# Order of the second block's weight loads and the transposed gradient tiles on one DMA queue

## The chip, the cores and the metric

One core of a Trainium2 chip runs the whole program in one launch. The metric is the device time of one execution in microseconds; the kernel before takes 1849.81 us (median of three runs, 1849.18 to 1849.89).

## The reference

The program computes a layer and all its gradients (a `vjp`). With x = A_q (2048 rows of 1024, bf16):

```
xn  = layernorm(x)
A   = xn * (longconv(kv, ssm_k) + kv * ssm_D),   kv = shortconv(k, shift_k) * v
B   = (relu(xn @ W_gate) * (xn @ W_up)) @ W_down            # 1024 -> 3584 -> 1024
out = x + A + B
grads of (A_q, A_k, A_v, shift_k, ssm_k, ssm_D, W_gate, W_up, W_down) for grad_out
```

## The kernel before, in words

TensorE (PE) works through branch B, and the matmuls of branch A (a long convolution by transforms) are woven in between from about 120 us on. Only the first 60 us matter for the change. They belong to `hidden`, which computes the hidden layer and its gradient in 14 blocks: two halves of the rows (8 tiles of 128 rows each) times 7 blocks of 512 hidden columns. A block `n` makes, for each row tile `s`,

- `gate` (tile `ps_g`): 8 matmuls of xnT[s], the transposed normalised rows, with `wg`, a block of W_gate in four pieces of 256 KB;
- `up` (`ps_u`): 8 matmuls of xnT[s] with `wu`, the block of W_up, likewise four pieces;
- `grad_row` (`ps_h`): 8 matmuls of goT[s], the transposed rows of grad_out, with `wdT`, the transposed block of W_down, four pieces again, of which piece q serves matmuls 2q and 2q + 1.

The results go over ScalarE and VectorE to the tiles `ru`, `ht` and `gh` and are stored as `h_d` and `ug_d`. A tile xnT or goT stays in its slot for all 7 blocks of a half, so these are loaded once, in the first block.

The first block (`n == 0`, `ahead` in the code) runs while the layernorm is still being made, row tile after row tile. xnT 0 to 5 are transposed on PE (`flip_xn`), xnT 6 and 7 by a DMA transpose from the layernorm's output in SBUF (`flip_xn`, last queued one kept in `self.turned`). All eight goT are DMA transposes from HBM (`load_T`): 0 to 3 are asked for before `hidden` begins, 4 to 7 in the loop over `sp`. The order of row tiles on PE, from 32.8 us, is: gradient of tiles 2, 3, 4, 5; gate and up of 6; gate and up of 7; gradient of 6 and 7. Then block 2 (`n == 1`) starts with gate of tiles 0 and 1, up of 0 and 1, gradient of 0 and 1.

There are four sets of weight buffers. The first block uses three of them. The second block's gate weights go into the spare set, so their load waits for no matmul. Its up weights go where the first block's gate weights were and its down weights where the first block's up weights were, so these loads wait for PE.

Nearly all loads are on the queue of SyncE (SP), which issues them one after the other. In the first block the stores of h, of the gradients and of xn go over GpSimd (POOL). The order on a queue comes from priorities that the code counts up (`Pri`), from pins to program order, and from `issue_after(ins)`, which places the instructions traced inside its block behind `ins` where both are on the same engine. In the kernel before, the lines are

```
while len(gT) < min(sp + 4, HS):
    with self.tc.issue_after(self.turned.ins if sp == 4 else self.copied.ins):
        gT.append(self.load_T(g, len(gT), "goT", HS + len(gT)))
```

where `self.copied` is a copy on ScalarE or VectorE, and further down `load_gate()` behind `self.stored`, which in the first block is a store on POOL. So the queue of SP holds in this stretch: goT 2, 3, the small load `sk_b`, wg (4 pieces), goT 4, 5, xnT 6, 7, goT 6, 7, wu (4), wdT (4).

Of the kernel before, what the change touches and what calls it, by code (L numbers as in the profile page):

```python
# [17 lines left out]
P = 128  # L18
# [30 lines left out]
class ABranch:  # L49
# [47 lines left out]
    def load(self, out, in_):  # L97
        self.pri.now()
        ins = self.nc.sync.dma_start(out=out, in_=in_)
        if self.pin:  # L100
            self.tc.keep_in_program_order(ins)
        else:
            self.pri.pin(ins)
# [776 lines left out]
class LnMlp:  # L880
# [292 lines left out]

    def load_T(self, src, st, name, slot, always=False):
        t = self.act_tile(name, slot)
        self.pri.pin(self.nc.sync.dma_start_transpose(out=t[:].rearrange("p (a b) -> p a b", b=P),
                                                      in_=src[st * P:(st + 1) * P, :]), always=always)
        return t

    def load_nat(self, src, st, name, slot):  # L1180
# [40 lines left out]
    def hidden(self, first, goT, load, ln, tables, Wg, Wu, Wd, g, xn_d, h_d, ug_d):  # L1221
# [6 lines left out]
        for n in range(N):  # L1228
            half, fb = divmod(n, self.FB)
            s0, cols, ahead = half * HS, slice(fb * 512, fb * 512 + 512), n == 0  # L1230
# [13 lines left out]
            def load_gate():  # L1244
                if last:
                    self.slab_part(h_d, 0, "hs", self.hs, 4, sg)
                else:
                    nw[0] = self.col_block(Wg, nb, "wg", to[0])
# [5 lines left out]
            def load_down(q):  # L1254
                if last and q == 0:
                    self.slab_part(h_d, 0, "hs", self.hs, 0, spare)
                elif not last:
                    if q == 0:
                        nw[2] = []
                    nw[2].append(self.row_piece_T(Wd, nb, "wdT", to[2], q, n == 1))  # L1260
# [105 lines left out]
            def gate_up(sp):  # L1366
                end = sp == HS - 2
                if ahead and not end:
                    gate(sp)
                    yield from step(self.PACE[0])  # L1370

                    def turn():
                        flip(sp + 2)
                        with self.tc.issue_after(self.copied.ins):
                            chunk()
                    up(sp, None, {4: turn})
                    yield from step(self.PACE[1])
                    gate(sp + 1)
                    yield from step(self.PACE[0])
                    up(sp + 1)  # L1380
                    yield from step(self.PACE[1])
                    return
                rows = [(f, s) for f in (gate, up) for s in (sp, sp + 1)]
                for f, s in sorted(rows, key=lambda r: r[1]) if ahead else rows:
                    f(s)
                    yield from step(self.PACE[f is up])
                    if end and f is gate and s == sp + 1:
                        (load_up if ahead else load_gate)()
                if end and ahead:
                    for q in range(4):  # L1390
                        load_down(q)
                elif end:
                    load_up()
                if swap:
                    next_rows(sp)
# [8 lines left out]
            def last_rows(sp):  # L1404

                self.hold = self.busy = True
                for q in range(2):
                    load_down(sp // 2 + q)

                def run(f, s):  # L1410
                    f(s)
                    yield from step(self.PACE[f is up])
                yield from run(gate, sp)
                yield from run(gate, sp + 1)
                yield from run(up, sp)
                yield from run(gate, sp + 2)
                yield from run(gate, sp + 3)
                load_gate()
                yield from run(up, sp + 1)
                yield from grad_row(sp)  # L1420
                yield from run(up, sp + 2)
                yield from run(up, sp + 3)
                load_up()
                self.busy = swap and not last
                if n == 1:
                    chunk()
                if swap:
                    next_rows(sp)
                    next_rows(sp + 2)
                for s in range(sp + 1, HS):  # L1430
                    yield from grad_row(s)
                if swap:
                    next_grads(sp)
                    next_grads(sp + 2)
# [37 lines left out]
            def grad(sp):  # L1472
                for s in (sp, sp + 1):
                    at = 3 if sp == 0 else 0
                    yield from grad_row(s, {at: lambda: flip_ahead(sp)} if ahead and s == sp + 1 else {})
                if swap:
                    next_grads(sp)

            def chunk(steps=3):
                with self.tc.issue_after(self.ln_act.ins):  # L1480
                    for _ in range(steps):
                        next(ln)
# [7 lines left out]
            for sp in range(0, HS, 2):  # L1490
                self.pri.now()
                while len(gT) < min(sp + 4, HS):
                    with self.tc.issue_after(self.turned.ins if sp == 4 else self.copied.ins):
                        gT.append(self.load_T(g, len(gT), "goT", HS + len(gT)))
                if ahead or sp < HS - 4:
                    if not ahead:
                        load_down(sp // 2)
                        yield from gate_up(sp)
                        if n == 4 and sp == 2:
                            for k in filter(self.bare, range(HS)):  # L1500
                                xT[k] = self.load_T(xn_d, k, "xnT", k)
                        if sp:
                            self.hold = False
                        elif fb:
                            self.busy = False
                    if not ahead or sp != 4:
                        yield from grad(sp)
                    if ahead and sp == 2:
                        yield from grad(4)
                elif sp == HS - 4:  # L1510
                    yield from last_rows(sp)
                if ahead:
                    with self.tc.issue_after(self.stored.ins):
                        if sp == 0:
                            load_gate()
                if ahead and sp in (2, 6):
                    with self.tc.issue_after(self.put.ins):
                        for put in self.kept[0:4] if sp == 2 else self.kept[4:8]:
                            put()
                if ahead and sp == 6:  # L1520
                    with self.tc.issue_after(self.sent.ins):
                        load(6)
                if ahead and sp + 4 < HS:
                    yield from gate_up(sp + 4)
                if n == 1 and sp < 4:
                    with self.tc.issue_after(self.stored.ins):
                        for i in ((7,), (8, 9))[sp // 2]:
                            load(i)
                if n == 1 and sp != 4:
                    chunk()  # L1530
                if ahead and sp == 4:
                    with self.tc.issue_after(self.ln_act.ins), self.tc.issue_after(self.ln_dve.ins):
                        tables()
# [477 lines left out]
```

## Time and profile before

| | |
|---|---|
| median of three runs | 1849.81 us |
| lowest, highest | 1849.18, 1849.89 us |
| profiled execution: its own time | 1849.04 us |
| profiled execution: span | 1847.3 us |
| PE busy | 1827.6 us, 99% of the span |
| VectorE (DVE), ScalarE (ACT), POOL busy | 1118.2, 647.1, 34.9 us |
| DMA, mean over the span | 187 GB/s |
| SP's queue (q1) | 71.5% of 16 engines' span |
| PE by the table of stretches, 10 to 50 us | 39.79 of 40 us busy |

The profile is one execution. "SPq" rows are issues on SP's queue: start, then how long SP took to issue them. A number in square brackets is idle time of the engine before that row, with what ended it. A matmul of 128x512 is shown with 379 ns, since its row lasts until its results are out; one follows another every 0.216 us. The DMA share counts packets in flight on 16 engines and can be above 1.

### The profile page before, as it was taken

To read this page: it belongs to the slowest core of one execution; us is meant where nothing else is said; L and a number is where in the kernel's file an instruction comes from. 1 tells how busy PE (TensorE), PEld (TensorE's weight loads), DVE (VectorE), ACT (ScalarE), POOL (GpSimd) and SP (SyncE) were. 2 spreads that over 40 slices of the span, in tenths; PEclk is the share of its full clock that TensorE was granted. 3 is DMA by queue.
4 is the path that set the end of the run, shared out by engine and by line. 5 is a ranking of instruction groups with operands and counts; after the bars stand their busy time and mean duration, and the time that the engine had idled before them with its cause. 6 is when DMAs were issued, how large, how long until landed. Compare 5 with 4: busy or idle time off the path is not lost.

```text
span 1847.3 us, 32176 instructions
## 1 busy us (share of the span) xinstructions
PE 1827.6 (99%) x12970; PEld 846.9 (46%) x13182; DVE 1118.2 (61%) x1652; ACT 647.1 (35%) x1218; POOL 34.9 (2%) x72
## 2 busy tenths in 40 slices
PE   9999999999999999999999999999999999999999
PEld 4444444444444444444444444444444544444444
DVE  6656898698789758585685767721222222566652
ACT  6644544545444454544544455320000000111100
POOL 2200000000000000000000000000000000000000
PEclk9999999999999999999999999999999999999999
DMA  9997769969857866639566445389999767799973
GB/s 257 289 223 176 175 174 228 211 167 211 186 154 207 234 165 155 171 104 267 132 160 166 143 117 161 106 239 243 248 254 249 178 143 172 171 210 215 201 157 75
DMA packets 749989, 345.97 MB, mean 187 GB/s; under 512 B 581272, under 2 KB 718480, under 8 KB 749840
## 3 DMA queue, kind: packets, MB, share of 16 engines
q1 hardware_dynamic: 736048, 312.18, 71.5%
q10 hardware_dynamic: 9632, 17.04, 2.9%
q0 software_dynamic: 4160, 14.68, 2.3%
q8 instruction: 103, 1.69, 0.4%
q14 instruction: 46, 0.38, 0.1%
HBM read 143.79 MB, written 103.83 MB: 134 GB/s over the span
## 4 chain that ended last, share of the span: by engine, by line
PE 98%; issue 1%; DMA 0%; ACT 0%; SPq 0%; DVE 0%; ACTq 0%
PE ps_x L1860 21%; PE ps_w L1561 20%; PE ps_h L1152 10%; PE ps_u L1152 10%; PE ps_o L1728 10%; PE ps_g L1152 10%; PE ps_d L1561 9%; PE ps_c L83 4%; PE ps_d L1577 1%; PE ps_w L1577 1%; PE ps_r L1762 0%; DMA wg<-in_B_W_gate_dram 0%; DMA wu<-in_B_W_up_dram 0%; PE ps_u L1320 0%; ACT ln_j L965 0%
## 5 line engine op out<-in xcount | busy, mean ns | idle before, releaser
L1561 PE MATMUL ps_w<-ugs,xn_nat 128*128 128x512 bf16 x1675 | 375.2, 379 | 4.7 <-issue 2.9
L87 ACT CAST arena<-ps_c 128x512 bf16<-128x512 f32 x576 | 293.8, 611 | 103.0 <-PE ps_c L83 102.7
L1152 PEld LDWEIGHTS <-xnT 128*128 128x128 bf16 x1760 | 168.7, 98 | 205.2 <-issue 5.0
L1561 PEld LDWEIGHTS <-xn_nat 128*128 128x128 bf16 x1728 | 165.3, 98 | 200.8 <-issue 6.1
L343 DVE STREAM_TRANSPOSE arena<-arena 128x1024 f32<-128x1024 f32 x96 | 179.4, 1934 | 112.2 <-ACT arena L87 101.7
L1152 PE MATMUL ps_h<-wdT,goT 128*128 128x512 bf16 x873 | 201.9, 379 | 1.2
L1152 PE MATMUL ps_u<-wu,xnT 128*128 128x512 bf16 x861 | 201.3, 379 | 1.2
L1152 PE MATMUL ps_g<-wg,xnT 128*128 128x512 bf16 x848 | 199.4, 379 | 1.5
L1860 PE MATMUL ps_x<-wuT,guT 128*128 128x512 bf16 x878 | 197.5, 379 | 1.0
L1860 PE MATMUL ps_x<-wgT,ggT 128*128 128x512 bf16 x878 | 197.3, 379 | 0.9
L1878 ACT ACTIVATE w<-xn,m 128x512 f32<-128x512 bf16 x32 | 24.3, 806 | 479.9 <-DVE m L1871 366.6
L1728 PE MATMUL ps_o<-wd,hT 128*128 128x512 bf16 (+1 forms) x879 | 186.7, 372 | 0.9
L1561 PE MATMUL ps_d<-g_nat,hs 128*128 128x512 bf16 x743 | 166.5, 379 | 2.6 <-issue 1.9
L1860 PEld LDWEIGHTS <-guT 128*128 128x128 bf16 x896 | 87.7, 98 | 105.7
L1860 PEld LDWEIGHTS <-ggT 128*128 128x128 bf16 x896 | 87.7, 98 | 105.5
L1152 PEld LDWEIGHTS <-goT 128*128 128x128 bf16 x896 | 86.6, 98 | 104.3 <-issue 1.0
L1728 PEld LDWEIGHTS <-hT 128*128 128x128 bf16 x896 | 87.7, 98 | 99.9
L1449 ACT CAST gh<-ps_h 128x512 bf16<-128x512 f32 x112 | 66.2, 592 | 185.3 <-PE ps_h L1152 170.2
L1564 ACT CAST wi<-ps_w 128x512 bf16<-128x512 f32 x108 | 64.5, 597 | 187.6 <-PE ps_w L1561 149.1
L1720 DVE TENSOR_TENSOR ya<-ya,xe 128x1024 bf16<-128x1024 bf16 x16 | 11.1, 692 | 182.4 <-DMA xe<-xn_d 182.4
L91 DVE TENSOR_TENSOR t<-arena 128x2048 bf16<-128x2048 bf16 x96 | 114.0, 1220 | 0.4
L1561 PEld LDWEIGHTS <-hs 128*128 128x128 bf16 x768 | 73.3, 98 | 88.3 <-issue 1.8
(152 smaller groups left out, 1424.5 us busy)
## 6 DMA issues: line engine op xcount, KB each, us to landing
ugs<-ug_d SPq DMA_DIRECT2D x112, 256.0 KB
ug_d<-ru SPq DMA_DIRECT2D x104, 256.0 KB
wu<-in_B_W_up_dram SPq DMA_DIRECT2D x56, 256.0 KB
hs<-h_d SPq DMA_DIRECT2D x56, 256.0 KB
out_dram<-wi SPq DMA_DIRECT2D x56, 256.0 KB
wg<-in_B_W_gate_dram SPq DMA_DIRECT2D x55, 256.0 KB
h_d<-ht SPq DMA_DIRECT2D x104, 128.0 KB
gt<-in_grad_out_dram SPq DMA_DIRECT2D x32, 256.0 KB
```

What stands on the lines that cost most here:

```text
L83: self.pri.pin(self.nc.tensor.matmul(out, lhsT=lhsT, rhs=rhs, start=start, stop=stop))
L87: self.pri.pin(self.nc.scalar.copy(out=out, in_=in_))
L91: self.pri.pin(self.nc.vector.tensor_tensor(out=out, in0=in0, in1=in1, op=op))
L343: self.pri.pin(self.nc.vector.transpose(out=df[:, c0:c0 + 32, :], in_=sf[:, c0:c0 + 32, :]))
L1152: self.pri.pin(self.nc.tensor.matmul(ps[:], lhsT=xT[:, kt * P:(kt + 1) * P], rhs=w(kt), start=(kt == 0), stop=(kt == self.DT - 1)), always ...
L1449: self.pri.pin(nc.scalar.copy(out=gh[:], in_=ps[:]), **kept)
L1561: self.pri.pin(self.nc.tensor.matmul(ps[:], lhsT=lhsT(st), rhs=rhs(st), start=(st == 0), stop=(st == self.ST - 1)))
L1564: self.pri.pin(self.nc.scalar.copy(out=out, in_=ps[:]))
L1577: self.pri.pin(self.nc.tensor.matmul(ps[i][:], lhsT=lhsT(i, st), rhs=rhs(i, st), start=(st == 0), stop=(st == self.ST - 1)))
L1728: nc.tensor.matmul(ps, lhsT=hT[:, kt, :], rhs=self.wd[:, kt, oc], start=(kt == 0), stop=(kt == self.FT - 1))
L1860: nc.tensor.matmul(ps, lhsT=T[:, kt, :], rhs=W[:, kt, oc], start=(i == 0), stop=(i == n - 1))
L1878: nc.scalar.activation(out=w[:, oc], in_=xn[:, oc], func=ACT.Identity, scale=m[:, 7:8], bias=m[:, 6:7])
```

## The change

In the first block, goT 4 and 5 are now placed behind the previous goT load on SP (`self.loaded`, set in `load_T`), no longer behind a copy on another engine, which gave no order on SP. The four loads of the second block's gate weights move from behind a store on POOL at `sp == 0` to behind the last goT load at `sp == 4`. The queue of SP becomes: goT 2, 3, `sk_b`, goT 4, 5, xnT 6, 7, goT 6, 7, wg (4), wu (4), wdT (4). The instructions and their order on the other engines are those of before.

```diff
     def load_T(self, src, st, name, slot, always=False):
         t = self.act_tile(name, slot)
-        self.pri.pin(self.nc.sync.dma_start_transpose(out=t[:].rearrange("p (a b) -> p a b", b=P),
-                                                      in_=src[st * P:(st + 1) * P, :]), always=always)
+        self.loaded = self.nc.sync.dma_start_transpose(out=t[:].rearrange("p (a b) -> p a b", b=P),
+                                                       in_=src[st * P:(st + 1) * P, :])
+        self.pri.pin(self.loaded, always=always)
         return t
...
                 while len(gT) < min(sp + 4, HS):
-                    with self.tc.issue_after(self.turned.ins if sp == 4 else self.copied.ins):
+                    with self.tc.issue_after((self.turned if sp == 4 else self.loaded).ins):
                         gT.append(self.load_T(g, len(gT), "goT", HS + len(gT)))
+                if ahead and sp == 4:
+                    with self.tc.issue_after(self.loaded.ins):
+                        load_gate()
...
-                if ahead:
-                    with self.tc.issue_after(self.stored.ins):
-                        if sp == 0:
-                            load_gate()
```

## The prediction

> **What bounds the kernel now.** I read the page's busy table first, then the chain, then the window of the change. Bound: TensorE.
>
> ```profile
> PE 1827.6 (99%) x12970; PEld 846.9 (46%) x13182; DVE 1118.2 (61%) x1652; ACT 647.1 (35%) x1218; POOL 34.9 (2%) x72
> ...
> PE 98%; issue 1%; DMA 0%; ACT 0%; SPq 0%; DVE 0%; ACTq 0%
> ```
>
> The span is 1847.3 us and PE is busy for 1827.6, so 19.7 us are idle in all. The table by stretches says how little of that lies near the change:
>
> ```profile
> 0.00:10.00 10.00, 8.28 (x68) 1.00 0.84 279
> 10.00:50.00 40.00, 39.79 (x205) 1.00 1.12 261
> 50.00:100.00 50.00, 49.74 (x228) 1.00 1.08 268
> ```
>
> (Columns: stretch, its length, PE busy and matmuls, granted clock, DMA share, GB/s.) From 10 to 100 us PE is idle for 0.47 us at full clock, while the DMA engines' share is above 1. So here a DMA order can lose much and win little. The timeline of PE gives the moments at which each operand is wanted:
>
> ```profile
> 32.82 7.07 PE L1152 MATMUL ps_h<-wdT,goT 128*128 128x512 bf16 x31
> 39.89 1.90 PE L1152 MATMUL ps_g<-wg,xnT 128*128 128x512 bf16 x8
> ...
> 46.81 3.62 PE L1152 MATMUL ps_h<-wdT,goT 128*128 128x512 bf16 x16
> 50.26 3.62 PE L1152 MATMUL ps_g<-wg,xnT 128*128 128x512 bf16 x16
> 53.71 3.62 PE L1152 MATMUL ps_u<-wu,xnT 128*128 128x512 bf16 x15
> 57.17 3.62 PE L1152 MATMUL ps_h<-wdT,goT 128*128 128x512 bf16 x16
> ```
>
> Sixteen matmuls take 3.45 us from row to row (50.26 to 53.71), 0.216 us each. Block 2 begins at 50.26 with the moved weights. The weight loads of TensorE show the one wait:
>
> ```profile
> 39.88 6.59 PEld L1152 LDWEIGHTS <-xnT 128*128 128x128 bf16 x32 [0.49 <-DMA xnT<-ln_x]
> ```
>
> Tile 6 of the transposed activations comes late. The 32 matmuls from 32.82 would have ended their issue at 32.82 + 32 x 0.216 = 39.73; the next came at 39.89: 0.16 us lost. Last, SP's queue:
>
> ```profile
> 26.43 2.61 SPq L1144 DMA_DIRECT2D wg<-in_B_W_gate_dram  x4
> 29.09 5.46 SPq L1176 DMA_TRANSPOSE goT<-in_grad_out_dram  x2
> 34.66 2.79 SPq L1188 DMA_TRANSPOSE xnT<-ln_x  x2
> 37.51 3.65 SPq L1176 DMA_TRANSPOSE goT<-in_grad_out_dram  x2
> 43.98 2.45 SPq L1144 DMA_DIRECT2D wu<-in_B_W_up_dram  x4
> 46.52 8.30 SPq L1170 DMA_TRANSPOSE wdT<-in_B_W_down_dram  x4
> ```
>
> SP stands still from 41.16 to 43.98, waiting for PE to free wu's buffers. For landings I paired the completion counts that the trace records, sixteen per DMA and in order of issue: wg 30.91 to 34.04, goT 4 and 5 at 35.71 and 37.45, xnT 6 and 7 at 39.84 and 41.49, goT 6 and 7 at 43.79 and 44.97, wu 49.79, 50.52, 51.23, 52.24, wdT 53.69, 55.26, 55.95, 56.99.
>
> **The change part by part.** The instruction orders of the two programs are equal on PE, ACT, DVE and POOL, with nothing added or removed. On SP the four wg loads (256 KB each) go from ahead of goT 4 to behind goT 7; six transposed loads move up past them. Waits on landings follow the operands; no engine gets a new one on work.
>
> *goT 4 and 5 earlier.* Issued from 26.43 instead of 29.09. PE wants them at 36.27 and 38.00 (32.82 plus 16 and 24 matmuls); they landed 0.56 before. Nothing waited, so the gain is nothing.
>
> *xnT 6 and 7 earlier.* They also wait for DVE's scaling (L998), which ends at 33.14 and 35.71. So xnT 6 is issued at about 33.2 instead of 34.66 and lands near 38.4 (issue end to landing was 3.9 us: 35.95 to 39.84), before 39.73. The 0.16 us goes. What is late next is xnT 7: issued near 35.8 instead of 36.06, wanted at 43.35, landed at 41.49: 1.9 us to spare.
>
> *goT 6 and 7.* SP's gain shrinks to between the 0.3 us of xnT 7 and, because goT 6 and 7 took 2.05 and 1.54 us to issue where an uncontended transpose takes 1.3, about 0.8. They end near 40.4 and land near 44.2, wanted at 46.81 and 48.54.
>
> *wg later.* Four issues of 2.61 us fit from 40.4 to 43.0, inside SP's standstill, so wu is still issued at 43.98: no cost in the sequencer. The cost is in the transfers. 1.05 MB at the mean that the DMA view gives for 40 to 56 us, 326 GB/s, is 3.2 us; the same four took 3.84 in their old place (30.20, the landing before them, to 34.04). Off that go 0.8 us by which the queue is ahead, and 0.4 us near 51.6 in which the engines moved little. I take 3.2 - 0.8 - 0.4 = 2.0 us by which all behind wg lands later; the bounds are 0 (the transfers freed early repay all) and 3.84 (no repayment).
>
> *What that meets.* wg lands one spacing ahead of wu's first: 49.79 + 2.0 - 0.73 = 51.06 for the last, wanted at 50.26 + 6 x 0.216 - 0.16 = 51.40. wu's last: 54.24, wanted at 54.85. The wdT pieces 0 to 3 are wanted at 57.01, 57.44, 57.87, 58.31 and land at 55.69, 57.26, 57.95, 58.99. The last is 0.7 us late. Slacks do not add: one wait shifts all later demands, so the total is shift less the smallest slack, 58.31 - 56.99 = 1.3 us. Stall: 2.0 - 1.3 = 0.7, between 0 and 2.5.
>
> Later waits: block 2's next weights are issued on PE's freeing of buffers (wu of the third block at 85.42), and land from 84.47 on for 91.70, so I cost the delay there at nothing; if that cover is gone, wu's last piece (94.82, wanted 96.45) has 1.6 us, itself moved by PE's own delay. SP's stores of h and of the gradients behind wdT are up to 2 us later; ScalarE's idle rows behind ug_d from 40 to 200 us are 3.0 us in two waits, beside PE's work.
>
> Sum: -0.16 + 0.7 = +0.5 us. The profiled execution took 1849.04 (1.74 around its span); 1849.6 on that scale. It lies 0.77 below the median of 1849.81, so 1850.3.
>
> [...]
>
> **The rivals.** *Hidden altogether* (no stall, only the gain): the shift stays under 1.3 us. For it: the lull in the DMA view of 34 to 44 us (slices of 0.25 us):
>
> ```profile
> DMA  9899999997999499990000299989999698999699
> GB/s 113 50 206 371 435 209 292 288 482 289 245 290 42 87 289 333 271 118 0 3 9 9 40 287 452 459 330 224 291 290 505 262 524 177 385 425 315 173 287 413
> ```
>
> Nothing moves from 38.5 to 39.5. If the earlier order closes this lull, a microsecond is repaid. Against: the lull stands ahead of xnT 6's landing and may move with it. Time: 1849.81 - 0.16 = 1849.65.
>
> *Slower, by slow transposes.* Issues of transposes take 1.3 us when free and 2 to 3.9 behind copies: wdT 0 and 1 took 2.79 and 2.63, ending as wu landed; 2 and 3 took 1.30. If eight copies instead of four ahead keep all four slow, wdT 3 loses 2 x 1.4 = 2.8 us beyond a shift of 3.2: 6.0 - 1.3 = 4.7, less 0.16: +4.5, 1854.3. It decides from a shift of 5.2 us on (1.3 + 0.16 + 3.7, where 3.7 us is the 0.2% that a measurement of this kernel can tell from no change). Against: wdT 2 and 3 became fast as soon as wu had landed, whoever stood before it.
>
> [...]
>
> *Faster by over 3.7 us.* PE would have to recover more than the 0.47 us that it is idle from 10 to 100 us; the rest of its idle time is in the start, ahead of the change, and in short gaps far behind.
>
> *The change not doing what it says* is excluded by the compiled order on SP.
>
> **How the numbers follow.** Small stall (+0.1 to +2.4): 0.52. Hidden: 0.27. Slower rival: 0.18. Faster: 0.03. The first two are within 0.2%, and so is a little of the third: 0.80 within, 0.17 slower, 0.03 faster. The low end is the hidden case less the spread of the three runs below their median (0.63): 1849.0. The high end is the stall's upper bound (1849.81 - 0.16 + 2.5 = 1852.2) with some of the slower rival: 1852.6.
>
> **What would show it.** Right: SP's row for wg near 40.4, no [0.49 <-DMA xnT<-ln_x] before the weight loads near 39.7, and a wait of TensorE on wdT of about 0.7 us near 58. Wrong towards hidden: PE's rows at 50.1, 53.55 and 57.0 with no wait. Wrong towards slow: the wdT row of SP over 11 us instead of 8.30, or a wait on wg near 50.1, which would mean that POOL's stores hold SP's queue harder than I took it.

## The result, and the profile after

The changed kernel takes 1855.53 us (median of six runs, 1855.47 to 1856.85) against 1849.28 us for the kernel before in the same comparison: 6.25 us more, ratio 1.0036, 95% interval 1.0025 to 1.0046. It is slower by more than the spread of the runs, and outside the range of 1849.0 to 1852.6 that was given. The profiled execution has a span of 1853.7 us, 6.4 us above the 1847.3 of before.

SP's queue after the change (start, time to issue):

```profile
26.22 4.51 SPq L1176 DMA_TRANSPOSE goT<-in_grad_out_dram  x2
33.19 3.81 SPq L1189 DMA_TRANSPOSE xnT<-ln_x  x2
37.06 3.29 SPq L1176 DMA_TRANSPOSE goT<-in_grad_out_dram  x2
40.40 2.34 SPq L1144 DMA_DIRECT2D wg<-in_B_W_gate_dram  x4
43.83 3.67 SPq L1144 DMA_DIRECT2D wu<-in_B_W_up_dram  x4
47.60 11.41 SPq L1170 DMA_TRANSPOSE wdT<-in_B_W_down_dram  x4
```

The issues stand where the prediction put them: xnT 6 at 33.19, wg at 40.40, wu at 43.83. Two things are new. From 30.73 to 33.19 SP issues nothing, because xnT 6 waits for DVE; and the rows of wu and wdT have grown, from 2.45 to 3.67 and from 8.30 to 11.41 us.

PE's timeline (with idle time before a row, and what ended it):

```profile
39.75 1.89 PE L1152 MATMUL ps_g<-wg,xnT 128*128 128x512 bf16 x8
...
50.11 3.62 PE L1152 MATMUL ps_g<-wg,xnT 128*128 128x512 bf16 x16
53.56 3.76 PE L1152 MATMUL ps_u<-wu,xnT 128*128 128x512 bf16 x16
57.55 1.21 PE L1152 MATMUL ps_h<-wdT,goT 128*128 128x512 bf16 x4 [0.23 <-DMA wdT<-in_B_W_down_dram]
61.44 0.59 PE L1152 MATMUL ps_h<-wdT,goT 128*128 128x512 bf16 x2 [2.68 <-DMA wdT<-in_B_W_down_dram]
63.27 3.96 PE L1152 MATMUL ps_h<-wdT,goT 128*128 128x512 bf16 x10 [1.24 <-DMA wdT<-in_B_W_down_dram]
67.07 3.62 PE L1152 MATMUL ps_g<-wg,xnT 128*128 128x512 bf16 x16
```

The wait on xnT 6 is gone. The up row from 53.56 is 0.14 us longer than before, since wu's last piece lands at 54.96 where it is wanted at 54.86. All the rest is one gradient row: it waits for wdT piece 0, then 2, then 3. The next gate row starts at 67.07 and not at 60.62, 6.45 us later, and nothing changes behind it. In the kernel before:

```profile
60.62 3.62 PE L1152 MATMUL ps_g<-wg,xnT 128*128 128x512 bf16 x16
```

The last of these gradient rows holds a second loss: ten matmuls took 3.80 us to the next row (63.27 to 67.07) where they need 2.16. The table by stretches tells why (stretch, length, PE busy, granted clock, DMA share, GB/s):

```profile
60.00:62.00 2.00, 0.56 (x2) 1.00 1.03 362
62.00:64.00 2.00, 0.76 (x3) 0.81 1.12 325
64.00:66.00 2.00, 2.00 (x6) 0.50 1.25 210
66.00:68.00 2.00, 2.00 (x9) 0.84 1.07 398
```

The granted clock was 0.50 for (0.19 + 0.50 + 0.16) x 2 / 0.5 = 3.4 us, right behind the waits. So the profiled loss is -0.16 (xnT 6) + 4.96 (the last wdT piece used at 63.27, due at 58.31) + 1.64 (half clock) = 6.44 us, against 6.4 between the spans. This splits the profiled execution alone; its mean granted clock was 0.999, as in one other of the six runs, and 0.998 in the remaining four.

Landings, paired as in the prediction, say how wdT came to be so late. wu: 52.48, 53.49, 54.22, 54.96, each 2.7 to 3.0 us later than before. wdT: 57.51, 58.13, 61.40, 63.23, later by 3.8, 2.9, 5.4 and 6.2. Pieces 2 and 3 were issued from 54.85 to 59.00; POOL's second batch of four xn_d stores, 1 MB, was issued from 55.13 to 57.72 and landed from 60.27 to 62.64. In the kernel before, this batch began at 55.28, when all four wdT pieces were already issued (by 54.82), and the last wdT piece landed at 56.99. POOL's second batch, first in the kernel before, then in the changed one:

```profile
55.28 2.59 POOL L1001 DMA_DIRECT2D xn_d<-ln_x  x4
```
```profile
55.13 2.59 POOL L1001 DMA_DIRECT2D xn_d<-ln_x  x4
```

### The profile page after: what moved, and what is told of

Same layout as the page of the kernel before. It is cut to its first block, busy times and chain, and to the rows that moved or that the text cites. A ratio compares the mean times of both kernels' runs of the same rounds, so it can differ in the third digit from the quotient of the medians.

```text
span 1853.7 us, 32388 instructions
## 1 busy us (share of the span) xinstructions
PE 1845.2 (100%) x13182; PEld 847.6 (46%) x13182; DVE 1119.1 (60%) x1652; ACT 646.8 (35%) x1218; POOL 34.9 (2%) x72
## 4 chain that ended last, share of the span: by engine, by line
PE 99%; DMA 1%; ACT 0%; DVE 0%; SPq 0%; issue 0%
PE ps_x L1860 21%; PE ps_w L1561 20%; PE ps_h L1152 11%; PE ps_g L1152 10%; PE ps_u L1152 10%; PE ps_o L1728 10%; PE ps_d L1561 9%; PE ps_c L83 4%; PE ps_d L1577 2%; PE ps_w L1577 1%; PE ps_r L1762 0%; DMA wdT<-in_B_W_down_dram 0%; DMA ln_x<-in_A_q_dram 0%; PE ps_u L1321 0%; PE pst_x L1197 0%; PE ps_g L1321 0%
## 5 line engine op out<-in xcount | busy, mean ns | idle before, releaser
L1561 PE MATMUL ps_w<-ugs,xn_nat 128*128 128x512 bf16 x1728 | 381.1, 379 | 0.0
```

The lines of the kernel that those rows point to most:

```text
L1561: self.pri.pin(self.nc.tensor.matmul(ps[:], lhsT=lhsT(st), rhs=rhs(st), start=(st == 0), stop=(st == self.ST - 1)))
```

## The experiments

All but the last, which is the changed kernel itself, are edits of the changed kernel. The kernel before, measured beside them, took 1849.41 us (30 runs) for the first four and 1848.88 (17 runs) for the last three. Losses are counted from these.

The theory (A): behind SP's standstills for DVE, the gate weights' bytes come on top of wu and wdT; the late wdT pieces then meet POOL's second batch of stores; and the long wait brings the half clock. The rivals: transposes are issued slowly behind eight copies, whoever else is on the engines (B); the loss is the time of the moved bytes, wherever behind goT 4 and 5 they go (C); the place beside POOL's first batch and ahead of wu is to blame (D).

**The gate weights behind goT 5.** The goT half of the change stays; wg goes into SP's first standstill.

```diff
-                if ahead and sp == 4:
+                if ahead and sp == 2:
                     with self.tc.issue_after(self.loaded.ins):
                         load_gate()
```

> The four loads of the second block's gate weights stand behind the transposed gradient tiles 5, ahead of xnT 6; goT 4 and 5 are early as in the changed kernel. Theory A (in the changed kernel SP stands twice before xnT 6 and 7, from 30.73 to 33.19 and 35.06 to 35.77 us, with nothing queued that could move, so the gate weights' 1 MB comes on top of wu and wdT later; the last wdT pieces then meet POOL's second batch of xn stores, PE waits 5 us and the clock gate adds 1.65): the gate weights fill the first standstill, SP issues them from about 30.7 to 33.2, wdT lands as in the kernel before, PE waits at most 0.8 us near 39.8 on xnT 6; 1849 to 1850 us, granted clock 1.00. Theory C (any place behind goT 4 and 5 delays the weights by the time of their bytes): slower than before by several us, 1852 to 1856. Theory B (transposes are issued slowly when eight copies stand directly ahead of them): as A, for only four copies stand ahead of wdT.

Measured: 1849.66 us, ratio 0.9999 (0.9991 to 1.0008). SP's queue:

```profile
30.54 2.19 SPq L1144 DMA_DIRECT2D wg<-in_B_W_gate_dram  x4
32.89 5.75 SPq L1189 DMA_TRANSPOSE xnT<-ln_x  x2
...
46.51 7.79 SPq L1170 DMA_TRANSPOSE wdT<-in_B_W_down_dram  x4
```

wg fills the standstill, and the last wdT lands at 56.88, as before (56.99). PE waits 0.16 us on xnT 6 and for nothing else here. So bringing goT 4 and 5 forward costs nothing that these runs can tell, and neither does moving wg behind them: theory C falls. The DMA engines show the difference in the stretch 33.2 to 36 us: the first row is of the kernel before, the second of the changed one, the third of this one.

```profile
33.20:36.00 2.80, 1.00 1.20 261
```
```profile
33.20:36.00 2.80, 1.00 0.74 114
```
```profile
33.20:36.00 2.80, 1.00 1.13 347
```

With wg in the standstill the engines move 347 GB/s there; in the changed kernel 114. This place is also ahead of the eight stores of 256 KB that POOL issues from 36.3 us on, and no run separates that from the standstill being filled.

**The second batch of xn stores off POOL.** They go behind the last wdT piece on SP (`self.kept` holds the stores, now with the queue as an argument).

```diff
...
-                if ahead and sp in (2, 6):
+                if ahead and sp == 2:
                     with self.tc.issue_after(self.put.ins):
-                        for put in self.kept[0:4] if sp == 2 else self.kept[4:8]:
+                        for put in self.kept[0:4]:
                             put()
+                if ahead and sp == 6:
+                    with self.tc.issue_after(self.sent.ins):
+                        for put in self.kept[4:8]:
+                            put(nc.sync)
```

> The changed kernel, but the second batch of four xn stores (256 KB each) goes from POOL's queue to SP's, directly behind the last wdT piece. Theory A: wdT 0 and 1 land as in the changed kernel (57.5, 58.1), wdT 2 and 3 no longer beside POOL's stores, 1 us after one another, at about 59 and 60; PE waits 0.5 to 1.9 us in all, no half clock; 1850 to 1851.3 us. Theory B (slow transposes behind eight copies, whoever else is on the engines): SP's row for wdT stays near 11 us and the time at 1855.5. If the clock alone were the cause of the whole loss, it would be 1855.5 too.

Measured: 1851.09 us (1850.54 to 1852.90), ratio 1.0009 (1.0000 to 1.0018); granted clock 1.00 in every execution.

```profile
47.66 11.41 SPq L1170 DMA_TRANSPOSE wdT<-in_B_W_down_dram  x4
59.12 2.23 SPq L1001 DMA_DIRECT2D xn_d<-ln_x  x4
```
```profile
55.48 2.32 PE L1152 MATMUL ps_u<-wu,xnT 128*128 128x512 bf16 x10 [0.46 <-DMA wu<-in_B_W_up_dram]
58.02 0.61 PE L1152 MATMUL ps_h<-wdT,goT 128*128 128x512 bf16 x2 [0.22 <-DMA wdT<-in_B_W_down_dram]
59.14 0.59 PE L1152 MATMUL ps_h<-wdT,goT 128*128 128x512 bf16 x2 [0.52 <-DMA wdT<-in_B_W_down_dram]
60.17 0.59 PE L1152 MATMUL ps_h<-wdT,goT 128*128 128x512 bf16 x2 [0.44 <-DMA wdT<-in_B_W_down_dram]
61.21 2.32 PE L1152 MATMUL ps_h<-wdT,goT 128*128 128x512 bf16 x10 [0.45 <-DMA wdT<-in_B_W_down_dram]
```

The row of wdT is as long as in the changed kernel, 11.41 us, and yet the loss is 1.7 us and no longer 6.25. So a slow issue alone does not make the loss (theory B); most of it needs POOL's stores beside pieces 2 and 3. The pieces now land 1.0 to 1.1 us apart, and the waits, one on wu and four on wdT, bring no half clock. The ten matmuls behind the last take 2.15 us (61.21 to 63.36). What is left is the bytes on top: wu lands about 3 us and wdT 3.8 to 4.3 us later than before. The profiled execution, at 1852.38, is one of the longest; its waits delay the next gate row by about 3.2 us, more than the 0.5 to 1.9 expected and more than the median stands for. The expectation had wdT 2 and 3 at 59 and 60; they landed at 60.13 and 61.17.

**Two pieces and two.** `col_block` is written out for this load, so that two pieces go behind goT 5 and two behind goT 7.

```diff
...
-                if ahead and sp == 4:
+                if ahead and sp in (2, 4):
```

> Pieces 0 and 1 of the gate weights behind goT 5, pieces 2 and 3 behind goT 7 (the place of the changed kernel). Theory A: half the bytes come on top of wu and wdT, these land about 1.3 us later than before, wdT 3 near 58.3 where it is wanted, ahead of POOL's stores; PE waits 0 to 0.6 us, clock 1.00; 1849 to 1850 us: the loss is not in proportion to the bytes moved. Theory C (loss in proportion to the bytes moved): half the loss, 1852.4 us.

Measured: 1850.51 us, ratio 1.0006 (0.9997 to 1.0016).

```profile
57.04 1.46 PE L1152 MATMUL ps_h<-wdT,goT 128*128 128x512 bf16 x6
59.92 2.32 PE L1152 MATMUL ps_h<-wdT,goT 128*128 128x512 bf16 x10 [1.42 <-DMA wdT<-in_B_W_down_dram]
```

By the medians half the bytes cost 1.1 us of 6.25, far from half; the interval includes no loss at all. The profile shows a wait of 1.42 us, more than the 0 to 0.6 expected, and the time is above the 1849 to 1850 expected. One of the ten executions, the longest (1853.02 us), had a granted clock of 0.999. In the profile the wu pieces land 1.2 to 1.3 us later than in the kernel before. Three pieces of wdT are in time; only the last, issued from 54.73 to 56.01, still meets POOL's stores (from 55.15) and lands at 59.88.

**Filler in the waits.** Twenty extra matmuls into an unused bank keep PE at work while it would wait; their result is used nowhere.

```diff
...
+                if n == 1 and s == 0:
...
+                    after = {3: lambda: fill(14), 5: lambda: fill(6)}
                 self.gemm8(ps, gT[s], wd, None, after)
```

> The changed kernel with 20 extra matmuls whose result is not used (14 after matmul 3 and 6 after matmul 5 of block 2's first gradient row), 4.3 us of PE's time laid into its two long waits. If the half clock after the waits is what makes the ten matmuls behind them slow (1.65 us): granted clock 1.00, wdT 3 still near 63.2, PE's next gate row at about 65.5 instead of 67.07, time 1853.9 us. If the ten matmuls are slow for another reason (operands late): 1855.5 us, or more by what of the filler is not covered.

Measured: 1854.75 us (1853.55 to 1857.45), granted clock 1.00 in all seven executions.

```profile
57.92 3.18 PE L1450 MATMUL ps_junk<-wg,xnT 128*128 128x512 bf16 x14
60.94 0.59 PE L1152 MATMUL ps_h<-wdT,goT 128*128 128x512 bf16 x2
61.37 1.46 PE L1450 MATMUL ps_junk<-wg,xnT 128*128 128x512 bf16 x6
62.69 2.32 PE L1152 MATMUL ps_h<-wdT,goT 128*128 128x512 bf16 x10
64.84 3.62 PE L1152 MATMUL ps_g<-wg,xnT 128*128 128x512 bf16 x16
```

The last piece lands as late as in the changed kernel (at 62.64, 13.1 us behind block 2's first gate row in both), but the ten matmuls behind it take 2.15 us: the slow ten were the clock, and the profile is 1.9 us shorter (1851.8 against 1853.7), though that one is the shortest of the seven executions. The median fell by only 0.8 us where 1.6 was expected, and lies between the two expected times. The filler's 4.3 us are hidden only where the waits are that long, and the spread is 3.9 us; no run here splits that remainder further.

**The gate weights behind xnT 7, and between xnT 6 and 7.** Both move `load_gate()` with its order edges and nothing else.

```
behind xnT 7:   goT 4 5, xnT 6 7, wg, goT 6 7, wu, wdT
between:        goT 4 5, xnT 6, wg, xnT 7, goT 6 7, wu, wdT
```

> The changed kernel with the four gate loads one step earlier: behind xnT 7, ahead of goT 6 and 7 (issued from about 37.1 instead of 40.4 us). Theory A (what costs is that the loads stand behind both of SP's waits for DVE, so that the stretch from 30.7 to 35.8 us stays without them and their bytes come on top of wu and wdT): the same bytes still have to move after 37 us, wdT 3 lands near 62 to 63, 1854.5 to 1856 us. Theory D (what costs is their place beside POOL's first batch of xn stores, issued 42.1 to 44.4, and right ahead of wu): they land before those, wu and wdT as in the kernel before or half way, 1849.4 to 1851.5 us.

> The four gate loads between xnT 6 and xnT 7: the first wait for DVE (to 33.2 us) stays empty, the second is filled. Theory A: part of the stretch is used again; wdT lands 1 to 3 us later than in the kernel before, PE waits 0 to 2 us there; xnT 7 is issued after the loads at about 37 and still in time; 1849.8 to 1852 us, between the versions behind goT 5 and behind goT 7. Theory D: as the kernel before, 1849 to 1850 us.

Measured: 1854.23 us (1851.95 to 1860.76), ratio 1.0035 (1.0022 to 1.0049), and 1853.02 us (1850.30 to 1856.06), ratio 1.0020 (1.0011 to 1.0029). PE's waits, first behind xnT 7, then between:

```profile
49.61 5.18 PE L1153 MATMUL ps_h<-wdT,goT 128*128 128x512 bf16 x16 [2.98 <-DMA goT<-in_grad_out_dram]
```
```profile
46.13 1.90 PE L1153 MATMUL ps_g<-wg,xnT 128*128 128x512 bf16 x8 [3.34 <-DMA xnT<-ln_x]
...
52.51 1.90 PE L1153 MATMUL ps_h<-wdT,goT 128*128 128x512 bf16 x8 [1.02 <-DMA goT<-in_grad_out_dram]
```

Theory D falls: an earlier place, as long as it is behind the first standstill, still costs 5.4 and 4.1 us, against 6.7 for the changed kernel beside them. But the wait is not where theory A had it. It moves to the transposed load directly behind wg: goT 6, which landed at 49.56, or xnT 7, at 46.09, and wdT then has no wait. The first time is just below the 1854.5 to 1856 expected; for the place between, the expectation was too low by 1 us, since it held xnT 7 to be in time. Each of these loads, too, was in flight beside POOL's stores: behind xnT 7, goT 6 was issued by 42.98, and eight stores of 256 KB issued from 36.45 to 44.19 landed from 41.91 to 51.35. How much of the delay is wg's bytes and how much these stores, no run isolates.

**The changed kernel once more.**

> The changed kernel once more, to stand on the same chip beside the two versions above and to see whether its time goes with its clock: 1855 to 1857 us, granted clock below 1.00 in every execution, and a half clock of one stretch of 3.4 us right behind the wait on wdT.

Measured: 1855.60 us, ratio 1.0036 (1.0023 to 1.0049). Its five executions had a granted clock of 1.000, 0.999, 0.998, 0.998 and 0.998 and took 1853.41, 1854.86, 1855.60, 1856.68 and 1855.99 us. The first is the profiled one: waits of 1.84 and 1.63 us on wdT, no half clock, against the expectation of one every time.

```profile
60.61 0.59 PE L1152 MATMUL ps_h<-wdT,goT 128*128 128x512 bf16 x2 [1.84 <-DMA wdT<-in_B_W_down_dram]
62.83 2.32 PE L1152 MATMUL ps_h<-wdT,goT 128*128 128x512 bf16 x10 [1.63 <-DMA wdT<-in_B_W_down_dram]
```

A stretch of 3.4 us at half clock lowers the mean of an execution by 3.4 x 0.5 / 1854 = 0.0009.

## Why the prediction was wrong, point by point

- *What bounds the kernel; little to win, much to lose:* right. One caution: the 0.47 us of idle PE from 10 to 100 us was hardly idle time. The page of before lists 12970 matmuls, the page after 13182 for the same program, and missing records read as idle. With wg behind goT 5, where all 13182 are listed, PE is idle for 0.16 us in the same stretch. The true room was smaller still.
- *goT 4 and 5, xnT 6:* right. The 0.16 us came back, and nothing else did.
- *wg's issue at no cost in the sequencer:* right as far as wu's start, 43.83 us. The rows behind it took longer to issue, though: wu 3.67 us and wdT 11.41.
- *"All behind wg lands later" by 3.2 - 0.8 - 0.4 = 2.0 us:* the step that failed. For wu the shift was 2.7 to 3.0, so almost nothing was repaid. I counted the earlier queue as a repayment. DVE's end at 33.14 went into the issue times, but not into what the engines could move: the queue gets 2.9 us ahead (26.22 against 29.09), then waits 2.5 us for DVE, with wg no longer there to use the time. And the shift is not one number for all that follows: 3.8 us for the first wdT, 6.2 for the last, since pieces 2 and 3 slipped into POOL's second batch of stores. The last is far past the upper bound of 3.84. The prediction's sum had no term for that batch, which in the kernel before began 0.5 us behind wdT's last issue. A slack in landing time was compared with a shift, where the slack to the next traffic was what ran out.
- *Smallest slack sets the stall, 0.7 us:* the method holds (58.31 to 63.27 is 6.24 less 1.3), the size was 4.96.
- *The half clock:* the prediction's sum had no term for it. It cost 1.6 us in the profiled execution, where ten matmuls took 3.80 us instead of 2.16. A wait of 2.98 us (wg behind xnT 7) was followed by a half clock, and a wait of 3.34 us (between) was not, so in these traces the length of a wait alone does not tell. The last section has the waits side by side.
- *Slower, by slow transposes, 0.18:* the sign it named came, 11.41 us for wdT's row, and the time, 1855.53, is 1.2 us above its 1854.3. That nearness is chance, for the cause shown is another: with the same 11.41 us and POOL's stores elsewhere the time was 1851.09.

What stays open is the microsecond between wu's shift and wdT's in the kernel with the stores on SP, where no xn store is beside the pieces. Two ug_d stores of POOL's, issued from 50.51 to 54.91 and landed by 57.73 and 59.33, still are. No run isolates it.

## What to carry to other kernels

A load with slack, placed ahead of one that waits for compute, is what keeps a queue at work during that wait; move it behind, and its bytes add to the next rush nearly in full (wu 2.7 to 3.0 us later here, where 3.2 would be all of them). Before moving a transfer in a full stretch, list what other queues will issue within a few microseconds of each operand's new landing: with such small slacks the loss need not go in proportion to the bytes (here half of them cost 1.1 us of 6.25). And price a TensorE wait with a possible half clock on top: here one came behind waits of 2.98 us in one trace and of 2.68 and 1.24 us in another, where it cost 1.6 us.

## What the runs showed of the hardware

In two of the profiled executions the granted clock fell to 0.50 for 3.4 us as a wait of PE for a load ended: in the changed kernel from 63.2 to 66.6 us, and with wg behind xnT 7 between 46 and 54 us, where the granted clock of three stretches gives (4 x 0.08 + 2 x 0.50 + 2 x 0.20) / 0.5 = 3.4 us. In two others PE waited as well, and the granted clock stayed at 1.00:

| trace | PE's waits for loads there, us | PE busy | granted clock |
|---|---|---|---|
| changed kernel | 0.23, 2.68, 1.24 | 1.32 of 4 us (60 to 64) | 0.81 from 62 to 64, 0.50 from 64 to 66, 0.84 from 66 to 68 |
| wg behind xnT 7 | 2.98 | 1.02 of 4 us (46 to 50) | 0.92 from 46 to 50, 0.50 from 50 to 52, 0.80 from 52 to 54 |
| wg between xnT 6 and 7 | 3.34, then 1.02 | 0.80 of 4 us (42 to 46) | 1.00 from 42 to 54 |
| changed kernel once more | 1.84, 1.63 | 1.36 of 4 us (58 to 62) | 1.00 from 56 to 70 |

The longest of these waits, 3.34 us, brought no half clock. What decides whether it comes, no run here isolates. The changed kernel had it in its first profiled execution and not in the second; the second is one of five executions, which ran with a mean granted clock from 1.000 to 0.998 and took from 1853.41 to 1856.68 us.
